# One more chunk of u through block transposes and DRAM instead of TensorE, and an early split of the last batch's slot weights

## The chip, the cores and the metric

The kernel runs on one core of a Trainium2 chip. The core has a matrix engine (PE, whose weight loads appear as PEld), a vector engine (DVE), a scalar engine (ACT), a GpSimd engine (POOL) and SyncE (SP), which here issues nearly all transfers. Each engine executes its own instructions strictly in program order and waits on semaphores for the others. The metric is the device time of one execution in microseconds (us).

## What is computed

A spectral layer (real FFT over 3072 positions, a complex linear layer with a soft threshold, the inverse FFT) for 8 batches of 3072 tokens of 256 features, then a soft mixture of experts with 32 slots, then a dense layer with softmax gating and a layer norm. The change lies in the last part. Cut to that part, the reference is:

```
c = softmax(logits, axis=1)           # tokens x 32 slots
x = c @ slot_out                      # tokens x 256
h = x @ w_in                          # tokens x 1024
u = h * softmax(h, axis=1)
ln = (u - mean(u)) / sqrt(var(u) + 1e-6) * g_ln
out = ln @ w_out                      # tokens x 256
```

Everything is float32. For the large products the kernel splits a factor into a high part, rounded to the matrix engine's reduced float32 form, and a low part, which is the remainder.

## The kernel before

Phase 1 (up to about 655 us of the trace) does the spectral layer, the logits and the slot inputs, and leaves in a DRAM tensor `c_dram` the slot weights `c` of each batch, transposed, as a high and a low part. The last batch is stored once, unsplit.

Phase 2, the function `phase2`, then walks over the 24576 tokens in 192 tiles of 128 tokens. `i` counts tiles, `j` is a group of four tiles, `k` is a tile's place in its group. I call four tiles a round. The loop at its end writes out by hand, per iteration `i`, which tile each step works on; that order is the order on every engine:

- `hmat(i+2)` on PE: two matmuls of 512 columns give `hps`, the 1024 values of h for 128 tokens. `expo(i+1)` on ACT, `rowmax(i+2)` and `umul(i+1)` on DVE give the row minimum (of the negated h), the exponential, and the product `u`.
- `trans(i)` on PE turns the first four 128-column chunks of `u` into PSUM (`pu`, two buffers): four transposes. `uhi(i)` on ACT copies them rounded into `uh` (L1068); `ulo(i)` on DVE subtracts and writes `ul` (L1077).
- `blocks(i+1)` is the other way for the last four chunks. DVE transposes 32x32 blocks into `tb` (L1049), SP writes `tb` to DRAM as `td` (L1051). `sort(i)` reads it back (L1060), in an order that completes the transpose, into `t2`; the profile calls that tile `t`. Since `sort(i)` stands behind `blocks(i+1)`, a tile's read is issued after the next tile's write. `uhl2(i-2)` on POOL makes the high and the low part from it: a cast (L1086) and a subtraction (L1087).
- `vari(i)` on ACT squares; `rstd(i)` on POOL makes the scale factors, five small instructions once a round; `outp(i-4)` on ACT scales the result into `osb`, and once a round POOL adds its halves into `os` (L1143), which SP stores.
- `prod(i-3)` on PE: eight matmuls of 512 columns with the chunks of `uh`, then eight of 256 columns with the chunks of `ul`.

On POOL the order at a round's last iteration (`i%4 == 3`) is `uhl2` of the round's second tile, `rstd`, `os`; then `uhl2` of the third, the fourth, and the next round's first tile. I call the tile whose `uhl2` stands ahead of `rstd` and `os` A, and the one behind them B.

MB is the number of chunks that go by DRAM (4), MA the number that PE transposes. The rows of `w_out` lie in `wout_dram` in an order that depends on MB, written in phase 1 by `dec_rows` during the decoding of the weights. The last three tiles (`direct`) send no chunk through DRAM: POOL reorders the last four chunks into `ts` (L1046) and PE transposes them too, as a second group with the second `pu` buffer.

`pieces(j+2)` gives `hmat` the slot weights. For batches 0 to 6 they come from `c_dram` already split. For the last batch POOL makes the split in phase 2, per group: one cast of 128x512 (L978) and two subtractions of 32x512 (L981).

Of the kernel before, what the change touches and what calls it, by code (L numbers as in the profile page):

```python
# [35 lines left out]
def kernel(  # L36
# [99 lines left out]
    MB = 4  # L136
# [12 lines left out]
    def phase1(pl: ExitStack, pr_: ExitStack):  # L149
# [560 lines left out]
        def dec_rows(f, k, n, c):  # L710
            if n < MA:
                SP.dma_start(out=wout_dram[128 * n:128 * n + 128], in_=f[:, n - k, :])
                return
            v = wout_dram[128 * MA:1024].rearrange("(i b c) d -> b c i d", b=4, c=MB)
            for c in (c, c + 1):
                SP.dma_start(out=v[n - MA, c], in_=f[32 * c:32 * c + 32, n - k, :])
# [131 lines left out]
    def phase2(p2: ExitStack, pw: ExitStack):  # L848
        k_p = p2.enter_context(tc.tile_pool(name="k2_p", bufs=1))
        c_p = p2.enter_context(tc.tile_pool(name="c_p", bufs=2))  # L850
# [7 lines left out]
        def load_c(b, h):  # L858
            if b >= B:
                return  # L860
            t = c_p.tile([128, 32, 32], F32R, name="ct", tag="ct", bufs=3)
            for k in range(4):
                SP.dma_start(out=t[32 * k:32 * k + 32].rearrange("s a j -> s (a j)").bitcast(F32), in_=c_dram[b, 0 if b == B - 1 else k % 2, h])
            cts[b, h] = t
# [103 lines left out]
        def pieces(j):  # L968
            if j >= NG:
                return  # L970
            b, r = divmod(j, 6)
            h, ah = divmod(r, 2)
            src = cts[b, h][:, 16 * ah:16 * ah + 16, :].rearrange("p a j -> p (a j)")
            ctt[j] = src
            if b == B - 1:
                src = src.bitcast(F32)
                c4 = ctt[j] = c_p.tile([128, 512], F32R, name="c4", tag="c4")
                POOL.tensor_copy(out=c4, in_=src)  # L978
                for k in (1, 3):
                    z = slice(32 * k, 32 * k + 32)  # L980
                    POOL.tensor_tensor(out=c4[z], in0=src[z], in1=c4[z].bitcast(F32), op=ALU.subtract)  # L981
            if ah:
                c_todo[4 * j + 3] = (b + 1, h)
# [44 lines left out]

        def trans(i):
            if i >= NI:  # L1030
                return
            u = ut[i]
            for n, v in enumerate([u, u2t[i]] if direct(i) else [u]):
                ps = pu_p.tile([128, 4, 128], F32, name="pu", tag="pu")
                for k in range(4):
                    tp(ps[:, k, :], v[:, k * 128:(k + 1) * 128])
                ut[i, n] = ps


        def blocks(i):  # L1040
# [3 lines left out]
            if direct(i):  # L1044
                t = u2t[i] = u_p.tile([128, 512], F32, name="ts", tag="ts", bufs=2)
                POOL.tensor_copy(out=t.rearrange("p (c i b) -> p c i b", c=MB, b=4), in_=v.rearrange("p (b c i) -> p c i b", b=4, c=MB))  # L1046
                return
            t = u_p.tile([128, 512], F32, name="tb", tag="tb", bufs=2)
            DVE.transpose(out=t, in_=v)  # L1049
            d = t_d.tile([128, 512], F32, name="td", tag="td")  # L1050
# [4 lines left out]
        def sort(i):  # L1055
# [3 lines left out]
            t2 = u_p.tile([128, 4, 128], F32, name="t2", tag="t2", bufs=3)  # L1059
# [3 lines left out]
        def uhi(i):  # L1063
            if i >= NI:
                return
            uh = u_p.tile([128, 8, 128], F32R, name="uh", tag="uh")
            for n in range(2 if direct(i) else 1):
                ACT.activation(out=uh[:, 4 * n:4 * n + 4, :], in_=ut[i, n], func=AF.Copy)  # L1068
            uht[i] = [uh]

        def ulo(i):
# [3 lines left out]
            for n in range(2 if direct(i) else 1):  # L1075
                z = slice(4 * n, 4 * n + 4)
# [74 lines left out]

        c_todo = {}
# [16 lines left out]
        for i in range(NI + 4):  # L1169
# [6 lines left out]
            late_c(i)  # L1176
            trans(i)
# [153 lines left out]
```

## Time and profile before

| | |
|---|---|
| median of 3 runs | 1393.14 us (1391.06 to 1394.41) |
| the profiled execution | 1393.42 us, of which the span of the trace 1391.6 us |
| busy, share of the span | PE 96%, DVE 87%, PEld 81%, ACT 75%, POOL 67% |
| chain that ended last | PE 78%, DVE 9%, POOL 4%, issue 4% |

Shares of the whole span mix two phases. Phase 2 alone, from about 680 us, shows PE and DVE nearly without idle time. A view by stretches shows how busy each engine is there, the chain of waits shows whose instructions follow one another without a gap, and the timeline shows how long before its use each piece is ready.

### The profile page before, as it was taken

The page shows a single profiled execution, that of the slowest core. Times are in us where ns is not written, and L with a number is a line of the kernel's source. Part 1 is how long each engine was busy: PE and PEld are TensorE (multiplying, and loading weights), DVE is VectorE, ACT ScalarE, POOL GpSimd, SP SyncE. Part 2 cuts the span into 40 slices and gives each one's busy share as a digit, 9 for nine tenths or more (in the row PEclk, how much of TensorE's full clock was granted, in tenths as well). Part 3 has the DMA queues.
Part 4 walks back from the last instruction along what each step waited for, and adds up shares of the span by engine and source line. Part 5 has one row for each costly group of instructions (what it writes and reads, how often), then busy time and mean ns, then how long its engine had stood idle before and what let it go on. Part 6 is the DMA issues. An engine that isn't in the chain of part 4 may idle for free.

```text
span 1391.6 us, 28564 instructions
## 1 busy us (share of the span) xinstructions
PE 1331.2 (96%) x10012; PEld 1132.7 (81%) x10012; DVE 1217.5 (87%) x1885; ACT 1045.7 (75%) x2006; POOL 929.9 (67%) x963
## 2 busy tenths in 40 slices
PE   6999999999999998977899999999999999999998
PEld 3888888888888887854788888888888888888786
DVE  6777988887888889756999999999999999999995
ACT  5557676757666664433899999999999999999885
POOL 5557575757575644320577877878878878879996
PEclk8899999999999999989799999999999999999999
DMA  8865473637364562286465566665666665666552
GB/s 268 282 194 170 129 206 106 209 88 206 114 195 125 168 208 75 76 285 199 137 207 187 190 204 198 194 200 190 199 193 206 198 193 186 205 195 193 180 167 84
DMA packets 207774, 250.84 MB, mean 180 GB/s; under 512 B 15536, under 2 KB 148400, under 8 KB 207632
## 3 DMA queue, kind: packets, MB, share of 16 engines
q1 hardware_dynamic: 207296, 247.84, 57.3%
q8 instruction: 80, 1.31, 0.4%
q10 hardware_dynamic: 336, 1.18, 0.3%
q14 instruction: 62, 0.51, 0.1%
HBM read 141.09 MB, written 107.87 MB: 179 GB/s over the span
## 4 chain that ended last, share of the span: by engine, by line
PE 78%; DVE 9%; POOL 4%; issue 4%; DMA 2%; ACT 2%; SPq 0%; DVEq 0%; POOLq 0%; ACTq 0%
PE po L89 36%; PE pb L89 8%; PE hps L89 6%; PE pm L89 6%; PE pu L92 5%; PE s L89 5%; PE xps L89 4%; PE pa L89 3%; PE sps L92 2%; DMA xc<-in_x_dram 2%; PE pm L92 1%; POOL x L238 1%; DVE sl L316 1%; DVE yb L343 1%; DVE yb L342 1%
## 5 line engine op out<-in xcount | busy, mean ns | idle before, releaser
L89 PE MATMUL po<-gw,uh 128*128 128x512 f32 x1536 | 407.5, 407 | 3.5 <-POOL uh L1086 3.5
L89 PEld LDWEIGHTS po<-gw,uh 128*128 128x128 f32 x1536 | 274.7, 189 | 57.1 <-POOL uh L1086 6.0
L346 POOL TENSOR_TENSOR s<-yb,s 128x512 f32<-128x512 f32 x95 | 132.3, 1393 | 215.9 <-DVE s L345 190.2
L1005 DVE TENSOR_REDUCE st<-hps 128x1 f32<-128x1024 f32 x192 | 235.1, 1225 | 30.0 <-PE hps L89 10.7
L1087 POOL TENSOR_TENSOR ul<-t,uh 128x512 fp32r<-128x512 f32 x189 | 244.5, 1294 | 15.2
L1020 DVE SCALAR_TENSOR_TENSOR u<-hps,e 128x1024 f32<-128x1024 f32 x192 | 233.3, 1215 | 1.4 <-ACT e L1012 1.4
L89 PEld LDWEIGHTS po<-gw,ul 128*128 128x128 f32 x1536 | 207.7, 188 | 17.8
L1095 ACT ACTIVATE sq<-u,st 128x1024 f32<-128x1024 f32 x192 | 219.5, 1143 | 0.0
L1012 ACT ACTIVATE e<-hps,st 128x1024 f32<-128x1024 f32 x192 | 213.9, 1114 | 2.9 <-DVE st L1005 2.9
L89 PE MATMUL po<-gw,ul 128*128 128x256 f32 x1536 | 210.6, 279 | 0.0
L1086 POOL CAST uh<-t 128x512 fp32r<-128x512 f32 x189 | 115.8, 613 | 135.7 <-DMA t<-td 107.6
L238 POOL TENSOR_TENSOR x<-xc,x 96x512 fp32r<-96x512 f32 x120 | 162.7, 1365 | 32.8 <-ACT x L237 30.2
L1068 ACT ACTIVATE uh<-pu 128x512 fp32r<-128x512 f32 x195 | 116.7, 599 | 67.8 <-PE pu L92 57.3
L1136 ACT ACTIVATE osb<-po,st 128x512 f32<-128x512 f32 x192 | 130.7, 681 | 9.7 <-PE po L89 6.9
L1077 DVE TENSOR_TENSOR ul<-pu,uh 128x512 fp32r<-128x512 f32 x195 | 133.7, 686 | 3.6 <-ACT uh L1068 3.6
L1049 DVE STREAM_TRANSPOSE tb<-u 128x512 f32<-128x512 f32 x189 | 132.7, 702 | 0.0
L264 ACT ACTIVATE asb<-s 96x512 f32<-96x512 f32 x112 | 66.6, 595 | 74.4 <-PE s L89 74.4
L92 PEld LDWEIGHTS pu<-ident,u 128*128 128x128 f32 x768 | 96.5, 141 | 26.1 <-issue 0.8
L92 PE MATMUL pu<-ident,u 128*128 128x128 f32 x768 | 116.6, 275 | 0.0
L89 PE MATMUL s<-x,df_h 96*96 96x512 f32 x240 | 104.7, 438 | 12.3 <-ACT x L237 4.7
L89 PE MATMUL hps<-gst,ct 128*128 128x512 f32 x336 | 106.7, 400 | 10.0 <-DVE u L1020 8.6
L1143 POOL TENSOR_TENSOR os<-osb 128x1024 f32<-128x1024 f32 x47 | 113.4, 2413 | 0.0
(205 smaller groups left out, 2587.8 us busy)
## 6 DMA issues: line engine op xcount, KB each, us to landing
td<-tb SPq DMA_DIRECT2D x189, 256.0 KB, 2.1
t<-td SPq DMA_DIRECT2D x189, 256.0 KB, 3.1
apt<-ad SPq DMA_DIRECT2D x96, 256.0 KB, 4.1
out_dram<-os SPq DMA_DIRECT2D x47, 512.0 KB, 3.8
xc<-in_x_dram SPq DMA_DIRECT2D x56, 384.0 KB, 4.0
ad<-asb SPq DMA_DIRECT2D x56, 384.0 KB, 3.5
ct<-c_dram SPq DMA_DIRECT2D x96, 128.0 KB, 3.5
wt<-in_moe_w_dram SPq DMA_DIRECT2D x21, 512.0 KB, 8.5
```

The costliest lines, as they stand in the source:

```text
L89: PE.matmul(out=out, lhsT=lhsT, rhs=rhs, start=start, stop=stop)
L92: PE.transpose(out=out, in_=in_, identity=ident[0:k, 0:k])
L238: POOL.tensor_tensor(out=lo, in0=t, in1=hi.bitcast(F32), op=ALU.subtract)
L346: (DVE if (b, t) == (B - 1, NT - 1) else POOL).tensor_tensor(out=s, in0=yb, in1=s, op=ALU.subtract)
L1005: DVE.tensor_reduce(out=st[:, 0, k:k + 1], in_=hps[i], op=ALU.min, axis=AX.X)
L1012: ACT.activation(out=e, in_=hps[i], func=AF.Exp, bias=st[:, 0, k:k + 1], scale=-1.0, accum_out=st[:, 1, k:k + 1])
L1020: DVE.scalar_tensor_tensor(out=u, in0=hps.pop(i), scalar=1.0, in1=et.pop(i), op0=ALU.mult, op1=ALU.mult, accum_out=st[:, 2, k:k + 1])
L1049: DVE.transpose(out=t, in_=v)
L1077: DVE.tensor_tensor(out=ul[:, z, :], in0=ut.pop((i, n)), in1=uht[i][0][:, z, :].bitcast(F32), op=ALU.subtract)
L1087: POOL.tensor_tensor(out=ul[:, MA:8, :].rearrange("p c (a j) -> p c a j", a=4), in0=v, in1=w.bitcast(F32), op=ALU.subtract)
L1095: ACT.activation(out=sq, in_=ut.pop(i), func=AF.Square, bias=st[:, 2, k:k + 1], scale=-float(DFF), accum_out=st[:, 3, k:k + 1])
L1136: ACT.activation(out=o[:, k], in_=pot.pop(i), func=AF.Copy, scale=stt[j][:, 4, k:k + 1])
```

## The change

MB goes from 4 to 5: PE transposes three chunks of a tile, DVE, DRAM and POOL handle five. `tb`, `td` and `t2` grow from 512 to 640 columns, the ACT copy and the DVE subtraction shrink from 512 to 384. `dec_rows` writes w_out's rows in the order for five chunks, in 20 small stores (16 before) and three large ones (four before), in one more of the decoding's steps. The three direct tiles now use groups of 3, 3 and 2 transposes, with the same two `pu` buffers. The split of the last batch's weights no longer happens per group in the last batch. A new function `last_c`, called right after `late_c(i)`, loads the unsplit weights at iteration 20, splits them in four pieces of 96x256 on POOL at iterations 24, 26, 28 and 30, and stores both parts to `c_dram` at 33; `load_c` then reads them as for any batch. The pool that held the per-group copies has one buffer.

```diff
-    MB = 4
+    MB = 5
...
-                SP.dma_start(out=v[n - MA, c], in_=f[32 * c:32 * c + 32, n - k, :])
+                SP.dma_start(out=v[divmod(4 * (n - MA) + c, MB)], in_=f[32 * c:32 * c + 32, n - k, :])
...
-                SP.dma_start(out=t[32 * k:32 * k + 32].rearrange("s a j -> s (a j)").bitcast(F32), in_=c_dram[b, 0 if b == B - 1 else k % 2, h])
+                SP.dma_start(out=t[32 * k:32 * k + 32].rearrange("s a j -> s (a j)").bitcast(F32), in_=c_dram[b, k % 2, h])
...
-            if b == B - 1:
-                src = src.bitcast(F32)
-                c4 = ctt[j] = c_p.tile([128, 512], F32R, name="c4", tag="c4")
-                POOL.tensor_copy(out=c4, in_=src)
-                for k in (1, 3):
-                    z = slice(32 * k, 32 * k + 32)
-                    POOL.tensor_tensor(out=c4[z], in0=src[z], in1=c4[z].bitcast(F32), op=ALU.subtract)
...
+        def groups(i):
+            return ((0, MA), (MA, 6), (6, 8)) if direct(i) else ((0, MA),)
...
-            for n, v in enumerate([u, u2t[i]] if direct(i) else [u]):
+            for n, (z0, z1) in enumerate(groups(i)):
+                v, o = (u2t[i], MA) if n else (ut[i], 0)
...
-            d = t_d.tile([128, 512], F32, name="td", tag="td")
+            d = t_d.tile([128, 128 * MB], F32, name="td", tag="td")
...
-            t2 = u_p.tile([128, 4, 128], F32, name="t2", tag="t2", bufs=3)
+            t2 = u_p.tile([128, 4, 32 * MB], F32, name="t2", tag="t2", bufs=3)
...
+        def last_c(i):
+            d = [c_dram[B - 1, k].rearrange("h s x -> (h s) x") for k in range(2)]
+            if i == 20:
+                cl[0] = o_p.tile([96, 1024], F32R, name="cl", tag="cl", bufs=1)
+                cl[1] = o_p.tile([96, 1024], F32R, name="cl_h", tag="cl_h", bufs=1)
+                SP.dma_start(out=cl[0].bitcast(F32), in_=d[0])
+            elif i in (24, 26, 28, 30):
+                z = slice(128 * (i - 24), 128 * (i - 24) + 256)
+                POOL.tensor_copy(out=cl[1][:, z], in_=cl[0][:, z].bitcast(F32))
+                POOL.tensor_tensor(out=cl[0][:, z], in0=cl[0][:, z].bitcast(F32), in1=cl[1][:, z].bitcast(F32), op=ALU.subtract)
+            elif i == 33:
+                SP.dma_start(out=d[0], in_=cl[1].bitcast(F32))
+                SP.dma_start(out=d[1], in_=cl[0].bitcast(F32))
...
             late_c(i)
+            last_c(i)
```

PE in an ordinary tile of phase 2, before (`pu` is `trans`, `po` is `prod`, with the chunks of `uh` and `ul` as weights):

```order
L92 MATMUL pu<-ident,u 128x128 [waits PE_49]
L92 MATMUL pu<-ident,u 128x128 x3
L89 MATMUL po_10523<-gw,uh 128x512 [waits PE_49,Activation_49]
L89 MATMUL po_10523<-gw,uh 128x512 x3
L89 MATMUL po_10523<-gw,uh 128x512 [waits Pool_49]
L89 MATMUL po_10523<-gw,uh 128x512 x3
L89 MATMUL po_10523<-gw,ul 128x256 x4
L89 MATMUL po_10523<-gw,ul 128x256 [waits Pool_49]
L89 MATMUL po_10523<-gw,ul 128x256 x3
```

The same place after:

```order
L92 MATMUL pu<-ident,u 128x128 [waits PE_49]
L92 MATMUL pu<-ident,u 128x128 x2
L89 MATMUL po_10505<-gw,uh 128x512 [waits PE_49,Activation_49]
L89 MATMUL po_10505<-gw,uh 128x512 x2
L89 MATMUL po_10505<-gw,uh 128x512 [waits Pool_49]
L89 MATMUL po_10505<-gw,uh 128x512 x4
L89 MATMUL po_10505<-gw,ul 128x256 x3
L89 MATMUL po_10505<-gw,ul 128x256 [waits Pool_49]
L89 MATMUL po_10505<-gw,ul 128x256 x4
```

One transpose is gone, and PE's waits for POOL moved from the fifth to the fourth matmul of each kind.

PE in a direct tile at the end of phase 2, before (`ts` is POOL's reordered copy):

```order
L92 MATMUL pu<-ident,u 128x128 [waits DVE_49]
L92 MATMUL pu<-ident,u 128x128 x3
L92 MATMUL pu<-ident,ts 128x128 [waits DVE_49,Pool_49]
L92 MATMUL pu<-ident,ts 128x128 x3
L89 MATMUL po_18237<-gw,uh 128x512 [waits Activation_49]
```

The same place after:

```order
L92 MATMUL pu<-ident,u 128x128 [waits DVE_49]
L92 MATMUL pu<-ident,u 128x128 x2
L92 MATMUL pu<-ident,ts 128x128 [waits DVE_49,Pool_49]
L92 MATMUL pu<-ident,ts 128x128 x2
L92 MATMUL pu<-ident,ts 128x128 [waits DVE_49]
L92 MATMUL pu<-ident,ts 128x128
L89 MATMUL po_18003<-gw,uh 128x512 [waits Activation_49]
```

A third group with a wait of its own for DVE now stands between the transposes and the product.

POOL in the last batch, before (`c` is the split of the slot weights):

```order
L1087 TENSOR_TENSOR ul<-t_16669,uh 128x512 [waits PE_49,Pool_49]
L978 CAST c_16775<-ct 128x512 [waits DMAHW0_49]
L981 TENSOR_TENSOR c_16775<-ct,c_16775 32x512 [waits Pool_49]
L981 TENSOR_TENSOR c_16775<-ct,c_16775 32x512
L1086 CAST uh<-t_16721 128x512 [waits DVE_49,DMAHW4_49,PE_49,Pool_49]
```

The same place after:

```order
L1083 TENSOR_TENSOR ul<-t_16525,uh 128x640 [waits PE_49,Pool_49]
L1082 CAST uh<-t_16576 128x640 [waits DMAHW2_49,DVE_49,PE_49]
L1083 TENSOR_TENSOR ul<-t_16576,uh 128x640 [waits PE_49,Pool_49]
L1082 CAST uh<-t_16622 128x640 [waits DMAHW5_49,DVE_49,PE_49]
L1083 TENSOR_TENSOR ul<-t_16622,uh 128x640 [waits PE_49,Pool_49]
```

The three instructions of the split are gone from there, and the cast and subtraction of each tile are 640 columns wide.

## Rows read from the trace of the kernel before

**Rows 1.** Stretches: length, busy PE, PEld, DVE, ACT, POOL, granted clock, DMA share

```profile
1000.00:1100.00 100.00, 100.00 (x597) 86.63 (x596) 97.08 (x136) 92.04 (x165) 80.24 (x96) 1.00 0.62 196
1300.00:1340.00 40.00, 37.87 (x222) 31.87 (x221) 35.89 (x51) 34.03 (x61) 37.80 (x43) 1.00 0.55 178
```

**Rows 2.** Chain that ended last: start, length, engine, tile, line, instructions

```profile
754.78 2.80 PE po L89 x16
...
1264.46 2.80 PE po L89 x16
```

**Rows 3.** The same chain at 746 us, the transposes of one tile

```profile
746.96 0.44 PE pu L92 x4
```

**Rows 4.** Costliest groups between 700 and 1380 us: busy, mean ns, idle before

```profile
L1087 POOL TENSOR_TENSOR ul<-t,uh 128x512 fp32r<-128x512 f32 x181 | 234.2, 1294 | 14.5
...
L89 PE MATMUL po<-gw,ul 128*128 128x256 f32 x1456 | 199.4, 279 | 0.0
...
L1077 DVE TENSOR_TENSOR ul<-pu,uh 128x512 fp32r<-128x512 f32 x185 | 126.8, 686 | 3.6 <-ACT uh L1068 3.6
L1049 DVE STREAM_TRANSPOSE tb<-u 128x512 f32<-128x512 f32 x178 | 124.9, 702 | 0.0
...
L1086 POOL CAST uh<-t 128x512 fp32r<-128x512 f32 x180 | 110.3, 613 | 86.3 <-DMA t<-td 58.3 <-PE hps L89 9.9 <-PE pu L92 9.0
L1143 POOL TENSOR_TENSOR os<-osb 128x1024 f32<-128x1024 f32 x45 | 108.6, 2413 | 0.0
```

**Rows 5.** Timeline of an ordinary round, tiles A and B: start, length, instruction

```profile
901.31 0.70 DVE L1049 STREAM_TRANSPOSE tb<-u 128x512 f32<-128x512 f32 x1
...
906.17 0.37 SPq L1060 DMA_DIRECT2D t<-td  x1
...
909.40 0.61 POOL L1086 CAST uh<-t 128x512 fp32r<-128x512 f32 x1 [1.58 <-DVE tb L1049]
...
916.03 0.61 POOL L1086 CAST uh<-t 128x512 fp32r<-128x512 f32 x1
...
916.72 1.29 POOL L1087 TENSOR_TENSOR ul<-t,uh 128x512 fp32r<-128x512 f32 x1
...
918.99 1.09 PE L89 MATMUL po<-gw,ul 128*128 128x256 f32 x8
```

**Rows 6.** DMA issues between 800 and 1200 us: size, us to landing

```profile
td<-tb SPq DMA_DIRECT2D x108, 256.0 KB, 2.1
t<-td SPq DMA_DIRECT2D x108, 256.0 KB, 3.1
out_dram<-os SPq DMA_DIRECT2D x28, 512.0 KB, 3.8
```

**Rows 7.** Timeline of a round in the last batch

```profile
1335.07 0.62 POOL L1086 CAST uh<-t 128x512 fp32r<-128x512 f32 x1
...
1339.61 2.64 POOL L981 TENSOR_TENSOR c<-ct,c 32x512 fp32r<-32x512 f32 x2
...
1350.83 0.62 POOL L1086 CAST uh<-t 128x512 fp32r<-128x512 f32 x1
...
1351.51 1.20 PE L89 MATMUL po<-gw,uh 128*128 128x512 f32 x4 [0.69 <-POOL uh L1086]
1351.53 1.31 POOL L1087 TENSOR_TENSOR ul<-t,uh 128x512 fp32r<-128x512 f32 x1
...
1352.55 1.11 PE L89 MATMUL po<-gw,ul 128*128 128x256 f32 x8
```

**Rows 8.** Timeline at the direct tiles

```profile
1364.77 1.09 POOL L1046 COPY ts<-u 128x512 f32<-128x512 f32 x1
...
1366.33 2.11 PE L89 MATMUL po<-gw,uh 128*128 128x512 f32 x8
...
1367.54 1.28 DVE L1077 TENSOR_TENSOR ul<-pu,uh 128x512 fp32r<-128x512 f32 x2
...
1369.61 1.08 POOL L1046 COPY ts<-u 128x512 f32<-128x512 f32 x1
```

More of the change, by code (lines that the diff above doesn't have):

```diff
@@ L849, in phase2 @@
         k_p = p2.enter_context(tc.tile_pool(name="k2_p", bufs=1))
-        c_p = p2.enter_context(tc.tile_pool(name="c_p", bufs=2))
+        c_p = p2.enter_context(tc.tile_pool(name="c_p", bufs=1))
         gw = k_p.tile([128, 8, 2, D], F32R, name="gw")
@@ L1031, in trans @@
                 return
-            u = ut[i]
-            for n, v in enumerate([u, u2t[i]] if direct(i) else [u]):
+            for n, (z0, z1) in enumerate(groups(i)):
+                v, o = (u2t[i], MA) if n else (ut[i], 0)
                 ps = pu_p.tile([128, 4, 128], F32, name="pu", tag="pu")
-                for k in range(4):
-                    tp(ps[:, k, :], v[:, k * 128:(k + 1) * 128])
-                ut[i, n] = ps
+                for k in range(z0, z1):
+                    tp(ps[:, k - z0, :], v[:, (k - o) * 128:(k - o + 1) * 128])
+                ut[i, n] = ps[:, 0:z1 - z0]
         def blocks(i):
@@ L1044, in blocks @@
             if direct(i):
-                t = u2t[i] = u_p.tile([128, 512], F32, name="ts", tag="ts", bufs=2)
+                t = u2t[i] = u_p.tile([128, 128 * MB], F32, name="ts", tag="ts", bufs=2)
                 POOL.tensor_copy(out=t.rearrange("p (c i b) -> p c i b", c=MB, b=4), in_=v.rearrange("p (b c i) -> p c i b", b=4, c=MB))
                 return
-            t = u_p.tile([128, 512], F32, name="tb", tag="tb", bufs=2)
+            t = u_p.tile([128, 128 * MB], F32, name="tb", tag="tb", bufs=2)
             DVE.transpose(out=t, in_=v)
-            d = t_d.tile([128, 512], F32, name="td", tag="td")
+            d = t_d.tile([128, 128 * MB], F32, name="td", tag="td")
             SP.dma_start(out=d, in_=t)
@@ L1066, in uhi @@
             uh = u_p.tile([128, 8, 128], F32R, name="uh", tag="uh")
-            for n in range(2 if direct(i) else 1):
-                ACT.activation(out=uh[:, 4 * n:4 * n + 4, :], in_=ut[i, n], func=AF.Copy)
+            for n, (z0, z1) in enumerate(groups(i)):
+                ACT.activation(out=uh[:, z0:z1, :], in_=ut[i, n], func=AF.Copy)
             uht[i] = [uh]
@@ L1074, in ulo @@
             ul = u_p.tile([128, 8, 128], F32R, name="ul", tag="ul")
-            for n in range(2 if direct(i) else 1):
-                z = slice(4 * n, 4 * n + 4)
+            for n, z in enumerate(groups(i)):
+                z = slice(*z)
                 DVE.tensor_tensor(out=ul[:, z, :], in0=ut.pop((i, n)), in1=uht[i][0][:, z, :].bitcast(F32), op=ALU.subtract)
@@ L1150, in store @@
                 SP.dma_start(out=v, in_=os2)
+        cl = {}
+        def last_c(i):
[11 more added lines that the diff above has]
+                SP.dma_start(out=d[1], in_=cl[0].bitcast(F32))
         c_todo = {}
```

## The prediction

> **What bounds the kernel now.** I read the busy time by stretches first, since shares of the whole span mix two phases. In the middle of phase 2 PE is busy 100.00 of 100 us at a granted clock of 1.00 (2.4 GHz), DVE 97.08, POOL 80.24 [rows 1]. So PE bounds an ordinary tile, and DVE has only about 0.1 us of idle time in a tile. The chain of waits agrees: it is PE's own instructions without a gap, 509.68 us for 138 tiles, 3.693 us a tile [rows 2], 14.77 us a round of four. In the last batch the picture is another one: PE is busy 37.87 of 40 us and POOL 37.80 [rows 1]. There POOL never rests: a round on POOL takes 1350.83 - 1335.07 = 15.76 us, and PE waits for POOL's cast inside its product [rows 7]. The five rounds of this kind in the last batch are 1.0 us longer than an ordinary one.
>
> The last thing I read is how early POOL is. In an ordinary round tile A's block transpose starts on DVE at 901.31, SP issues its read at 906.17, POOL starts on it at 909.40, then does `rstd` and `os`, starts tile B at 916.03 and ends B's subtraction at 916.72 + 1.29 = 918.01 [rows 5]. PE starts the eight `ul` matmuls of B at 918.99. The steps between them are (1.09 - 0.28) / 7 = 0.116 us, with 0.28 for the last one's own length [rows 4], so the fifth, the first that needs POOL's part, comes at 919.45. That is 1.44 us later. Of these some 0.18 us are a hand-over that remains where PE does wait: POOL ends at 1351.53 + 1.31 = 1352.84 and the fifth matmul comes at 1352.55 + 4 x 0.119 = 1353.03 [rows 7]. So **POOL is 1.26 us early at tile B**, and earlier at the others, since only B stands behind `rstd` and `os`.
>
> **What each part costs.**
>
> *PE, one transpose less.* Four take 0.44 us of the chain [rows 3], so one is 0.11 us a tile, and PE's round becomes 14.77 - 0.44 = 14.33 us. The products keep their sixteen matmuls.
>
> *DVE.* The subtraction loses 128 columns and the block transpose gains 128. By their rows of 512 columns [rows 4] that is at most -686/4 = -172 ns and +702/4 = +176 ns; with a fixed part in each both are smaller and still equal. DVE's 97.08 us of work in 100 is 3.585 us a tile, 14.34 us a round: level with the new PE round, so DVE takes nothing back by itself, but there is nothing more to gain below 14.34. ACT's copy gets shorter, off the path.
>
> *POOL.* The trace has the subtraction at 512 columns (1294 ns) and a two-input addition at 1024 (2413 ns) [rows 4]: 2.19 ns a column, 0.28 us for 128. In proportion to 1294 it would be 0.32. The cast has one size here (613 ns): 0.15 us in proportion, some 0.13 with the same fixed share. Together +0.41 to +0.48 us a tile; I take 0.44, the middle. Is POOL then the bound? Its full round of 15.76 less the last batch's split (2.64 for its two subtractions and a 128x512 cast like L1086's 0.61 ahead of them, 3.3) is 12.4 us [rows 7]; plus 4 x 0.44 gives 14.2. It just fits into 14.34.
>
> *Transfers.* Write and read grow by 64 KB. The write is covered, because a read is issued only after the next tile's write. The read's 3.1 us [rows 6] lie on POOL's path. Bounds for the growth: nothing, if the same number of longer packets takes the same time, and 0.78 us in proportion to size. The nearest rows are the SP stores of 256 KB (2.1) and 512 KB (3.8) [rows 6], 0.42 us for 64 KB if all of it is transfer; the DMA engines are busy 0.62 of the time [rows 1], so a part is idle capacity. I take 0.25. The Trainium skill ("DMA: Bandwidth & Descriptors", "Anatomy of one DMA") gives about 2.0 us and bytes over 436 GB/s, which is 0.15 us for 64 KB and 2.6 us for 256 KB; the store of 256 KB here takes 2.1, so the trace does not carry that fit. With 0.15 the sum below would end at 1384.
>
> *POOL's lead at tile B.* All of this meets in the 1.26 us. POOL now does two longer tiles (A and B) between the read and the use: -0.88. The read lands later: -0.25. PE needs the data sooner: from A's block transpose to B's `ul` matmuls lie five PE periods, each 0.11 shorter; one comes back since the read waits for the next tile's write, one period later (-0.44). B's own transposes are one fewer (-0.11), and the first chunk from POOL is the fourth, not the fifth (-0.12). Sum -1.80: the lead becomes **-0.54 us, so PE waits**. A wait of PE in one round moves that round's PE times by as much, but the next round's tile A was transposed before it, so the next deadline is later by the same amount: lateness 0.54 is paid about every other round, 0.27 us a round on average. What is late next is B's `ul`; behind the waiting matmul on PE stand the next `hmat` and, through it, DVE and ACT. The round becomes 14.33 + 0.27 = 14.60 us.
>
> *The last batch's split.* Its 3.3 us a round go, and with them the five rounds that are 1.0 us longer: -5.0. In their place come four casts and four subtractions of 96x256, by half the cast (0.31) and 1.29 - 0.56 for the subtraction about 1.04 us each pair, 1.12 with the gaps that POOL's rows show between instructions, 4.5 us in two rounds. Two of the four pairs stand directly ahead of a tile B. POOL's room is 14.60 - 14.2 = 0.4 us a round; some 1.1 us are absorbed by the time it has caught up, and 3.4 us reach PE (bounds 2.0 and 4.5). The three transfers of 384 KB are issued by SP ahead of a write and a read; I count them in that range.
>
> *The tail.* A direct tile now has three groups for two PSUM buffers, so the third must wait until DVE has subtracted the first. Before, the second group is through and the product starts at 1366.33, while DVE does the two subtractions of that tile only from 1367.54 [rows 8], behind the next `umul`. The first ends 0.64 us later; then come the third group and the product, about 1368.4: +2.0 us. The next direct tiles also wait for POOL, whose copies lie 4.84 us apart [rows 8] and will lie 0.27 (the copy) + 0.44 further apart; by the third that is about 2.1 in all, not on top of the first. I take 2.1 (bounds 1.0 and 3.5).
>
> *Phase 1.* Four more small stores on SP, one more decoding step: no wait of another engine hangs on them, nothing.
>
> **Sum.** About 45 rounds times (14.60 - 14.77) = -7.7; the split out of the last batch -5.0; the early split +3.4; the tail +2.1. Together -7.2 us on the profiled execution's 1393.42, which is 0.28 above the median: **1386 us**.
>
> **Rivals.**
>
> *All hidden.* If POOL's lead is larger than I make it (the read no slower, PE's wait not formed), the round is 14.34, DVE's bound: 45 x -0.43 = -19.4, -5.0, +2.5 with more room on POOL, +2.1: 1374. For it: POOL's demand of 14.2 fits. Against: even with no slower read and 0.41 a tile the lead is 1.26 - 0.82 - 0.67 = -0.23.
>
> *Given back exactly.* A wait of 0.44 a round (lateness 0.88) leaves the round at 14.77; -5.0, then +3.4 to 4.5 and +2.1 remain: 1394.
>
> *Slower: POOL's path becomes longer than PE's old round.* With 0.48 a tile and a read 0.78 slower, the lead is 1.26 - 0.96 - 0.78 - 0.67 = -1.15, the wait 0.57, the round 14.90: 45 x 0.13 = +5.9, -5.0, +4.5 as POOL has no room, +3.5: 1402. It decides from a lateness of about 0.95 on. For it: the read's landing varies between tiles and a late one at A is paid in full. Against: no row shows 64 KB costing so much. The Trainium skill ("GPSIMD Engine Reference", "Engine selection") speaks against moving elementwise work to this engine, about twice as slow with two inputs; the same 512-column subtraction takes 1294 ns on POOL and 686 on DVE here, so the trace agrees on the engine's time. By that rule this rival would be the rule's outcome, 1402.
>
> **Chances.** Forecast (1380 to 1390) 0.47, hidden 0.20, given back 0.16, slower 0.17. About 0.2% (2.8 us) is what a measurement of this kernel can tell from no change; so faster 0.66, same 0.17, slower 0.17. The range 1375 to 1400 takes in most of the hidden case and of the slower one, and leaves out about 0.2.
>
> **What would show it.** Right: PE's chain in phase 2 shows three transposes a tile and a wait for POOL's `ul` at tile B, some 0.3 us a round, often in alternate rounds; the last batch's rounds are like the others; POOL is busy 95% or more; around tiles 24 to 31 PE loses 2 to 4 us; a direct tile's third group waits for DVE. A round of 14.34 without waits of PE would show the lead mis-sized. Longer `t` reads than 3.4 us, or a subtraction over 1.6 us, would show the slower case. Wrong altogether: a DVE whose 640-column transpose costs much more than 0.88 us would make DVE the bound.

## The result: 0.6% slower, and where the time went

The changed kernel takes 1400.0 us (median of five runs, 1398.34 to 1401.76), the kernel before 1392.14 in the same comparison: a ratio of 1.0057, 95% interval 1.0042 to 1.0071. The forecast was 1386, and the direction was wrong. The profiled execution took 1401.76 us, with a span of 1400.0.

The page of the kernel after: busy time and share of the span by engine, then the chain that ended last by engine.

```profile
PE 1326.8 (95%) x9823; PEld 1114.6 (80%) x9823; DVE 1218.4 (87%) x1888; ACT 1027.2 (73%) x2009; POOL 986.9 (70%) x953
...
PE 54%; DVE 17%; POOL 12%; DMA 7%; issue 6%; ACT 4%; SPq 0%; POOLq 0%; DVEq 0%; ACTq 0%
```

PE has 189 matmuls less, and yet the chain is no longer PE's own: PE's share fell from 78% to 54%, and POOL and DMA, which were at 4% and below, are now 12% and 7%. The same two stretches as in [rows 1], after (columns as there):

```profile
1000.00:1100.00 100.00, 98.77 (x569) 83.76 (x568) 96.13 (x136) 88.35 (x163) 89.45 (x96) 1.00 0.74 229
1300.00:1340.00 40.00, 39.73 (x231) 33.83 (x230) 38.51 (x54) 35.20 (x65) 35.81 (x39) 1.00 0.66 211
```

In the middle of phase 2 PE now has idle time; POOL went from 80 to 89, the DMA engines from 0.62 to 0.74. In the last batch the loss is gone (PE 37.87 to 39.73). The waits between 700 and 1390 us (engine, line, releaser, us in total, times, longest) name the ones that have grown:

```profile
POOL uh L1082 <- DMA t<-td: 31.2, 38, 2.5
DVE st L998 <- PE hps L89: 25.9, 35, 1.8
PEld po L89 <- POOL uh L1082: 25.0, 34, 1.9
PE po L89 <- POOL uh L1082: 10.9, 17, 1.4
```

The same three of DVE and PE in the kernel before, between 700 and 1380 us:

```profile
DVE st L1005 <- PE hps L89: 6.5, 7, 1.1
PEld po L89 <- POOL uh L1086: 6.0, 6, 1.1
PE po L89 <- POOL uh L1086: 3.5, 5, 0.7
```

PE waits for POOL's cast, and DVE then waits for PE's `hps`, as the prediction had it behind the waiting product. An ordinary round of after, tiles A and B as in [rows 5] (timeline: start, length, engine, line, instruction, idle time before it):

```profile
908.45 0.83 DVE L1045 STREAM_TRANSPOSE tb<-u 128x640 f32<-128x640 f32 x1
...
913.33 0.37 SPq L1056 DMA_DIRECT2D t<-td  x1
...
917.28 0.72 POOL L1082 CAST uh<-t 128x640 fp32r<-128x640 f32 x1 [0.66 <-DMA t<-td]
...
921.94 2.41 POOL L1139 TENSOR_TENSOR os<-osb 128x1024 f32<-128x1024 f32 x1
...
924.30 0.72 POOL L1082 CAST uh<-t 128x640 fp32r<-128x640 f32 x1
...
925.07 1.00 PEld L89 LDWEIGHTS po<-gw,uh 128*128 128x128 f32 x5 [0.33 <-POOL uh L1082]
925.10 1.58 POOL L1083 TENSOR_TENSOR ul<-t,uh 128x640 fp32r<-128x640 f32 x1
...
926.35 1.25 PE L89 MATMUL po<-gw,ul 128*128 128x256 f32 x8
```

A's block transpose starts at 908.45 and POOL has A's data at 917.28, 8.83 us later; before it was 909.40 - 901.31 = 8.09 [rows 5]. POOL is idle for 0.66 us until then, works without a gap through `rstd`, `os` and B, and ends B's subtraction at 925.10 + 1.58 = 926.68. B's eight `ul` matmuls, of which the last five need it, have begun at 926.35 and take 1.25 us in place of 1.09.

Where the 8.3 us of the two spans come from, worked out as the start of the same tile's first product in the one trace and the other:

| stretch | change, us | forecast |
|---|---|---|
| up to tile 4 (phase 1 and start) | +2.73 | 0 |
| tiles 4 to 20 | +0.03 | -0.7 |
| tiles 20 to 40 (early split) | +4.51 | +2.5 |
| tiles 40 to 160 (30 rounds) | +3.10 | -5.1 |
| tiles 160 to 185 (last batch) | -5.55 | -6.0 |
| tiles 185 to 188 (direct tiles) | +3.55 | +2.1 |
| the rest | -0.04 | 0 |

Over tiles 48 to 151 a PE period without a wait is 3.594 us (3.693 before), so a round without waits would be 14.374. The round is 14.863: a wait of 0.49 us a round, where the forecast had 0.27.

### The profile page after: what moved, and what is told of

The parts are those of the page before. It is cut to its first block, busy times and chain, and to the rows that moved or that the text cites. A ratio compares the mean times of both kernels' runs of the same rounds, so it can differ in the third digit from the quotient of the medians.

```text
span 1400.0 us, 28198 instructions
## 1 busy us (share of the span) xinstructions
PE 1326.8 (95%) x9823; PEld 1114.6 (80%) x9823; DVE 1218.4 (87%) x1888; ACT 1027.2 (73%) x2009; POOL 986.9 (70%) x953
## 4 chain that ended last, share of the span: by engine, by line
PE 54%; DVE 17%; POOL 12%; DMA 7%; issue 6%; ACT 4%; SPq 0%; POOLq 0%; DVEq 0%; ACTq 0%
PE po L89 20%; PE pb L89 7%; PE pm L89 6%; PE s L89 5%; POOL os L1139 4%; PE xps L89 4%; DMA t<-td 3%; PE hps L89 3%; DVE u L1013 3%; PE pa L89 3%; DVE st L998 3%; DMA xc<-in_x_dram 3%; POOL ul L1083 2%; POOL uh L1082 2%; PE sps L92 2%
## 5 line engine op out<-in xcount | busy, mean ns | idle before, releaser
L89 PE MATMUL po<-gw,uh 128*128 128x512 f32 x1536 | 415.8, 410 | 11.9 <-POOL uh L1082 11.2
L1083 POOL TENSOR_TENSOR ul<-t,uh 128x640 fp32r<-128x640 f32 x189 | 297.2, 1573 | 15.2
L89 PE MATMUL po<-gw,ul 128*128 128x256 f32 x1536 | 216.1, 282 | 0.0
L1082 POOL CAST uh<-t 128x640 fp32r<-128x640 f32 x189 | 136.1, 720 | 84.1 <-DVE tb L1045 44.8
L1064 ACT ACTIVATE uh<-pu 128x384 fp32r<-128x384 f32 x198 | 97.0, 490 | 91.0 <-PE pu L92 84.9
L1045 DVE STREAM_TRANSPOSE tb<-u 128x640 f32<-128x640 f32 x189 | 157.8, 835 | 0.0
L89 PE MATMUL hps<-gst,ct 128*128 128x512 f32 x384 | 122.0, 400 | 10.6 <-DVE u L1013 9.2
L1073 DVE TENSOR_TENSOR ul<-pu,uh 128x384 fp32r<-128x384 f32 x198 | 108.9, 550 | 5.0 <-ACT uh L1064 4.8
L89 PEld LDWEIGHTS xps<-d_sb,apt 128*128 128x128 f32 x768 | 99.6, 194 | 13.5 <-issue 2.9
L89 PE MATMUL xps<-d_sb,apt 128*128 128x128 f32 x768 | 106.0, 281 | 1.4 <-DMA apt<-ad 1.3
```

Source lines behind the costliest of these rows:

```text
L89: PE.matmul(out=out, lhsT=lhsT, rhs=rhs, start=start, stop=stop)
L1082: POOL.tensor_copy(out=w, in_=v)
L1083: POOL.tensor_tensor(out=ul[:, MA:8, :].rearrange("p c (a j) -> p c a j", a=4), in0=v, in1=w.bitcast(F32), op=ALU.subtract)
```

## The experiments

All medians, each against the kernel before on the same chip; "wait" is the round over tiles 48 to 151 less four PE periods without a wait (14.374, or 14.773 with four chunks); the next two columns are changes against the kernel before in the traces.

| kernel | median us | ratio (95%) | wait a round | tiles 20 to 40 | tiles 185 to 188 |
|---|---|---|---|---|---|
| after | 1400.0 | 1.0057 (1.0042, 1.0071) | 0.49 | +4.51 | +3.55 |
| e1_five_only | 1412.3 | 1.0137 (1.0114, 1.0159) | 0.53 | +0.77 | +2.65 |
| e2_early_only | 1388.8 | 0.9961 (0.9948, 0.9973) | 0.00 | +0.97 | -0.16 |
| e3_short_read | 1392.3 | 0.9990 (0.9978, 1.0001) | 0.25 | +4.79 | +3.57 |
| e4_os_later | 1382.2 | 0.9917 (0.9898, 0.9936) | 0.18 | +2.25 | +3.55 |
| e5_split_start | 1378.0 | 0.9881 (0.9866, 0.9895) | 0.12 | -0.49 | +3.26 |
| e6_two_groups | 1378.2 | 0.9887 (0.9870, 0.9903) | 0.12 | -0.74 | +3.84 |
| e7_short_pool | 1390.1 | 0.9966 (0.9953, 0.9979) | 0.21 | +4.93 | +2.65 |
| e8_long_read | 1394.5 | 1.0009 (0.9998, 1.0021) | 0.01 | 0.00 | +0.16 |
| e9_spread_c | 1377.4 | 0.9886 (0.9870, 0.9902) | 0.01 | -0.24 | +3.56 |
| e10_tail | 1373.5 | 0.9862 (0.9848, 0.9875) | 0.04 | -1.01 | +0.90 |
| e11_store_k0 | 1376.1 | 0.9881 (0.9867, 0.9895) | 0.04 | +0.01 | +0.91 |
| e12_four_best | 1389.2 | 0.9975 (0.9963, 0.9987) | 0.05 | +1.09 | +0.36 |
| e13_dec_steps | 1373.1 | 0.9850 (0.9830, 0.9869) | 0.05 | +0.38 | +0.94 |

**The two parts apart.** e1 is the changed kernel with the old split of the last batch:

```diff
+            if b == B - 1:
+                src = src.bitcast(F32)
+                c4 = ctt[j] = c_p.tile([128, 512], F32R, name="c4", tag="c4")
+                POOL.tensor_copy(out=c4, in_=src)
...
-            last_c(i)
```

> The first part of the change alone: five chunks by DRAM, but the last batch's weights are split per group in the last batch, as before. In the changed kernel the steady rounds were about 0.1 us longer than before (tiles 40 to 160: +3.1 us in 30 rounds), the tail cost +3.5, the start +2.7. If the early split is what cost the +4.5 us around tiles 20 to 40, those go here; the last batch has POOL at about 13.95 + 3.3 = 17.25 us a round against 15.76 before, five rounds, +7.5. Sum by this reading: 1392 + 2.7 + 4 (rounds) + 7.5 + 3.5, about 1407 to 1410. Rival, that the longer rounds come from somewhere else than POOL's path (PE or DVE): the last batch then costs no more than before, and the time is about 1392 + 2.7 + 4 + 3.5 = 1402.

Measured 1412.3, above the 1407 to 1410 expected: the last batch lost 9.9 us in place of 7.5. The +4.5 of tiles 20 to 40 go to +0.77 without the early split, and in the last batch tiles 160 to 185 take 9.86 us longer than before. That is 107.4 us for 6.25 rounds, 17.2 a round, which is POOL's own work as expected (17.25). A stretch of the last batch in e1 (columns as in [rows 1]):

```profile
1300.00:1340.00 40.00, 35.96 (x197) 28.85 (x196) 34.12 (x47) 30.91 (x56) 37.84 (x40) 1.00 0.55 175
```

POOL is as busy there as before (37.80), and PE falls from 37.87 to 35.96. So five chunks need the early split, or lose more than they win.

e2 has MB = 4 and direct groups `((0, MA), (MA, 8))`, with `last_c`.

> The second part alone: four chunks by DRAM as before, the last batch's weights split early. POOL is 1.26 us ahead of PE at tile B before, and a pair of early pieces takes 0.40 + 0.73 = 1.13 us on POOL in the changed kernel. If the +4.5 us around tiles 20 to 40 were POOL's lateness, the pieces are hidden here: 1392 - 5.0 + 0 to 1.5, that is 1387 to 1389. If the three transfers of 384 KB cost it (by holding up the reads), some 2 to 4 us of it remain: 1389 to 1391. If the +2.7 us at the start of the changed kernel come from the early split's side (its loads or stores in phase 1), they show here too; by the reading that they vary from kernel to kernel without a cause in phase 2, they need not.

Measured 1388.8: -5.17 us in the last batch, as forecast, and +0.97 at tiles 20 to 40. The POOL pieces are nearly hidden where POOL has a lead: of the 0.97 us, 0.25 lie in the round from tile 24 on and 0.72 in the round from tile 32 on, whose transfers stand behind the two stores of 384 KB. The same pieces and stores cost 4.1 in the changed kernel (4.51 less the ordinary 0.09 a round). Over an ordinary wait of 0.49, the rounds from tiles 20, 24 and 28 on are there 1.36, 1.34 and 0.26 us longer and the round behind the stores 1.60, while the next one waits for nothing. So more than a third of the cost comes with the stores and not with POOL's pieces. The timeline shows PE's weight loads waiting behind the two pieces that stand directly ahead of a tile B:

```profile
759.46 1.00 PEld L89 LDWEIGHTS po<-gw,uh 128*128 128x128 f32 x5 [1.85 <-POOL uh L1082]
775.70 0.98 PEld L89 LDWEIGHTS po<-gw,uh 128*128 128x128 f32 x5 [1.87 <-POOL uh L1082]
```

**The read's length and POOL's work apart.** e3 reads 512 of the 640 columns, into one of three tiles that were filled with zeros once:

```diff
-            t2 = u_p.tile([128, 4, 32 * MB], F32, name="t2", tag="t2", bufs=3)
-            SP.dma_start(out=t2, in_=d.rearrange("(a i) (b x) -> (i b) a x", a=4, b=4))
+            t2 = t2s[i % 3]
+            SP.dma_start(out=t2[:, :, 0:128], in_=d.rearrange("(a i) (b x) -> (i b) a x", a=4, b=4)[:, :, 0:128])
...
```

> The changed kernel, but the read from DRAM fetches only 512 of the 640 columns (the rest of the tile keeps zeros, so a fifth of five chunks is left out of the result); the write, POOL's cast and subtraction, DVE and PE keep their sizes. Theory 'the read lands later': A's data came 0.77 us later than in the kernel before against PE's need, and the wait of 0.47 us a round is half of a lateness of 0.93. With a read of the old size the lateness falls to between 0.16 and 0.43, the wait to 0.08 to 0.22, 0.25 to 0.39 us a round less in some 43 rounds: 1400 - 11 to 17, that is 1383 to 1389. Rival 'POOL's own work': if POOL has no room left (13.95 us of work a round), the earlier data only make POOL idle elsewhere and the time stays within 1397 to 1401.

Measured 1392.3, 7.7 under the changed kernel: a larger gain than the rival allowed (1397 to 1401) and a smaller one than the theory said (1383 to 1389). The round is 0.24 us shorter, just under the theory's 0.25 to 0.39, and the early split's cost did not shrink with it.

e8 is the opposite: the kernel before, moving 640 columns:

```diff
-            d = t_d.tile([128, 512], F32, name="td", tag="td")
+            d = t_d.tile([128, 640], F32, name="td", tag="td")
...
-            t2 = u_p.tile([128, 4, 128], F32, name="t2", tag="t2", bufs=3)
+            t2 = u_p.tile([128, 4, 160], F32, name="t2", tag="t2", bufs=3)
...
```

> The kernel before with transfers of 640 columns: the block transpose, PE and POOL keep their 512 columns, but write and read move 128x640 (a fifth of it zeros; the columns are not in the right places for the result). It measures the read's growth alone. Theory 'the landing grows by itself, with bytes and load': the median from issue to landing goes from 3.1 to 3.5 or 3.6, A's data come 0.4 to 0.7 later, the lead at B falls from 1.26 to 0.6 to 0.9, and PE still does not wait: 1391.5 to 1394.5. Rival 'the read is later because PE's waits delay its issue': the landing stays within 0.15 of before. If the time itself rises by over 3 us, the larger traffic costs something that no theory here has.

Measured 1394.5 (ratio 1.0009, interval with 1.0 in it): no change of the time, since POOL's lead covers it. Its transfers between 800 and 1200 us (size, us from issue to landing), to hold against [rows 6]:

```profile
td<-tb SPq DMA_DIRECT2D x108, 320.0 KB, 2.4
t<-td SPq DMA_DIRECT2D x108, 320.0 KB, 3.7
out_dram<-os SPq DMA_DIRECT2D x27, 512.0 KB, 4.5
```

The changed kernel has the same 2.4 and 3.7. For tile A alone, the mean of 26 reads from issue to landing is 3.16 us before, 3.82 in e8, 3.90 in the changed kernel and 3.35 in e3. So nearly all of the read's growth (0.66 of 0.74) comes with the bytes: it needs no wait of PE and no longer POOL work. e8 enlarges the write too; e3, with the larger write and the old read, tells them apart: 0.55 of the 0.74 go with the read's own size.

e7 is the complement of e3: full transfers, but POOL handles only four chunks.

```diff
-            v = t2t.pop(i).rearrange("p a (c j) -> p c a j", c=MB)
+            v = t2t.pop(i).rearrange("p a (c j) -> p c a j", c=MB)[:, 1:MB]
...
```

> The changed kernel with its full transfers, but POOL casts and subtracts only four of the five chunks (512 columns); the product uses the fifth chunk in place of the fourth, which is left out of the result. The complement of e3, where the read alone was shortened (landing 0.4 to 0.55 us earlier, round 0.26 shorter). Theory 'the two terms add up to one lateness': POOL's two tiles between A's landing and B's end shorten by 2 x 0.386, the lateness falls from 0.93 to 0.16, the wait from 0.47 to about 0.1 a round, 0.37 x 43 = -16; with POOL's room the early split costs 1 to 2 in place of 4.5, -3; sum 1381, range 1379 to 1386. Rival 'a floor of DVE and PE': e4 without POOL's order stayed at 14.55 a round, so the round comes down by 0.29 at most: 1400 - 12 - 3 = 1385 or more.

Measured 1390.1, 9.9 under the changed kernel, where the theory said 14 to 21. The wait fell to 0.21, not 0.1, and tiles 20 to 40 still cost 4.93. The round came down by 0.28, which is also what the rival, a floor of DVE and PE near 14.55, allowed (0.29); e9's round of 14.38, below, rules that floor out. The 4.93 are mostly one event: the round from tile 32 on takes 5.08 us more than without waits, and without this the early split would cost about 1 us, as the theory had it (1 to 2). Behind the two stores of 384 KB at iteration 33 the writes of tiles 34 and 35 take 5.88 and 4.81 us (2.4 otherwise), their reads go out late, PE waits, and then runs at a lower clock:

```profile
796.00:800.00 4.00, 3.47 (x20) 2.56 (x18) 3.42 (x6) 1.31 (x3) 3.50 (x7) 1.00 0.81 261
800.00:803.00 3.00, 0.96 (x3) 0.48 (x3) 1.63 (x2) 2.75 (x5) 3.00 (x3) 1.00 0.65 187
803.00:808.00 5.00, 4.84 (x20) 4.25 (x21) 1.94 (x5) 2.25 (x6) 4.76 (x6) 0.66 0.71 236
```

PE is busy for 0.96 of 3 us, and in the next 5 us the granted clock is 0.66 in the mean, between the levels of 2.4 and 1.2 GHz. The same round of the changed kernel takes only 2.09 us more.

**POOL's order.** e4 moves one instruction of 2.41 us on POOL behind tile B:

```diff
-                POOL.tensor_tensor(out=os2, in0=o[:, :, 0, :], in1=o[:, :, 1, :], op=ALU.add)
-                o_todo[i + 2] = (v, os2)
+                os_wait.append((i, v, o))
...
+        def addh():
+            if os_wait:
...
+                POOL.tensor_tensor(out=os2, in0=o[:, :, 0, :], in1=o[:, :, 1, :], op=ALU.add)
+                o_todo[i + 3] = (v, os2)
...
             uhl2(i - 2)
+            addh()
```

> The changed kernel, but the once-a-round addition that makes os on POOL (2.41 us) stands behind tile B's cast and subtraction, no longer ahead of them; its store goes out one iteration later. Nothing else. Theory 'lateness at one tile': POOL has 13.95 us of work in a round of 14.37, so it fits; only B was late, by 0.93. B now gains 2.41 us, the next tile loses 2.41 and gains a tile period 3.59 and still has about 0.3 to spare. The waits go, the round is 14.37 (four PE periods of 3.59), 0.47 less in some 43 rounds: 1380, range 1377 to 1385. Rival 'POOL has no room': the wait moves from B to the tile behind it and the time is 1396 to 1401. Rival 'DVE is the floor': waits go from the chain, but the round stays at 14.6 or more, as DVE's own work and its waits fill it: 1389 to 1393.

Measured 1382.2: the range of the first theory, 18 us under the changed kernel and 11 under the kernel before, with the same work on every engine. The ordinary stretch (columns as in [rows 1]):

```profile
1000.00:1100.00 100.00, 100.00 (x584) 85.94 (x584) 99.48 (x140) 91.96 (x167) 92.20 (x96) 1.00 0.77 236
```

Its waits between 850 and 1260 us:

```profile
PEld po L89 <- POOL uh L1082: 5.0, 10, 0.9
```

The same in the changed kernel:

```profile
PEld po L89 <- POOL uh L1082: 14.0, 23, 1.1
```

Between 1000 and 1100 us PE is busy 100 of 100 us again, with POOL at 92 and DVE at 99.5; between 1100 and 1200 it is 99.3. The round over tiles 48 to 151 is 14.55, not 14.37: the waits that are left fall into every second round (0.36 us in an odd round, 0.00 in an even one). Those are the rounds in which SP issues the four loads of the next slot weights, and there the reads of the third and fourth tile mostly take 5 to 6 us.

e9 spreads these loads (after e5, which follows):

```diff
-                load_c(*c_todo.pop(i))
...
+                    c_part.extend((b, h, k) for k in range(4))
+            if c_part:
+                b, h, k = c_part.pop(0)
+                SP.dma_start(out=cts[b, h][32 * k:32 * k + 32].rearrange("s a j -> s (a j)").bitcast(F32), in_=c_dram[b, k % 2, h])
```

> The kernel e5_split_start with the four transfers of 128 KB that load the next slot weights issued one per iteration, in four iterations, in place of all four in one. In e4 and e5 PE's wait for POOL falls only in every second round, the rounds in which these loads are issued (in e4 0.36 us in an odd round, 0.00 in an even one; in e5 0.23 and 0.00), and there the reads of the third and fourth tile take 5 to 6 us in place of 3.3 to 3.9. Theory 'the loads hold up the reads': the waits of odd rounds go for the most part, 0.115 us a round in some 40 rounds, -3 to -5: 1373 to 1375. Rival 'the 512 KB store of the output does it', one iteration ahead of them and unchanged here: less than 1.5 us is won, 1376.5 to 1379.

In the trace the theory holds: between 850 and 1260 us the wait is 0.3 us in all, where e5, which differs only in these loads, has 3.2. The 512 KB store, the rival, is unchanged.

```profile
PEld po L89 <- POOL uh L1082: 0.3, 2, 0.2
```

The round is 14.38. The median (1377.4, runs from 1374.0 to 1379.1) does not show it against e5's 1378.0 and lies in the rival's range (1376.5 to 1379): from tile 4 to the end the profiled execution gains 2.94 us, and its tile 4 comes 3.45 us later than in e5. By time alone e9 is open, by the waits it is shown.

**The early split.** e5 is e4 with the split in the time in which POOL does nothing (627 to 667 us):

```diff
-            elif i in (24, 26, 28, 30):
...
+            if i < 0:
+                cl[0] = o_p.tile([128, 768], F32R, name="cl", tag="cl", bufs=1)
...
+        last_c(-1)
         hmat(0)
```

> The kernel e4_os_later, but the last batch's weights are loaded and split before the first tile of phase 2, in one cast and one subtraction over 128x768; the stores stay at iteration 33. In e4 POOL does nothing from 627 to 667 us. Theory 'the early split costs what POOL does not have': tiles 20 to 40 of e4 lost 2.25 us against the kernel before, where the rounds around them gain about 1.0; with the two instructions (some 0.9 + 1.9 us) in the idle time, that 3.3 us goes: 1382.2 - 3.3 = 1379, range 1377.5 to 1380.5. Rival 'the three transfers of 384 KB cost it': two of them still fall at tile 33, so more than half stays: 1381 to 1382.5.

The two instructions on POOL in e5's timeline, behind 28.79 us without work:

```profile
655.78 0.82 POOL L1164 CAST cl_h<-cl 128x768 fp32r<-128x768 f32 x1 [28.79 <-DMA cl<-c_dram]
656.69 1.81 POOL L1165 TENSOR_TENSOR cl<-cl,cl_h 128x768 fp32r<-128x768 f32 x1
```

Measured 1378.0, 4.2 under e4. Tiles 20 to 40 go from +2.25 to -0.49, so POOL's pieces were the larger part. The stores at iteration 33 stayed; with ordinary waits taken off they cost 0.9 here.

**The direct tiles.** e6 makes two groups in place of three:

```diff
-            return ((0, MA), (MA, 6), (6, 8)) if direct(i) else ((0, MA),)
+            return ((0, 4), (4, 8)) if direct(i) else ((0, MA),)
```

> The kernel e5_split_start, but a direct tile makes two groups of four transposes (the fourth of the first group from ts) in place of three groups of 3, 3 and 2. Theory 'the third group waits for DVE': in e4 the third groups wait 2.07 and 0.65 us for DVE's subtraction; the waits go. POOL then sets the tail: its copies ts lie 5.47 us apart in e4 (4.84 before), so 1.3 us of the tail's 3.55 stay, and 2.2 go: 1.5 to 2.5 us less than e5. Rival 'POOL sets the tail already': less than 0.7 us is won.

Measured 1378.2, nothing won: the wait for DVE went, and a longer one for POOL's copy came (timeline at the second direct tile):

```profile
1355.55 1.33 PE L92 MATMUL pu<-ident,ts 128*128 128x128 f32 x5 [3.83 <-POOL ts L1042]
1356.53 3.76 PE L89 MATMUL po<-gw,uh 128*128 128x512 f32 x8
```

The product takes 3.76 us in place of 2.11 [rows 8]; the granted clock between 1355.5 and 1360 us was 0.50, after 3.83 us without an instruction of PE. So the tail needs POOL's order mended as well. e10 is e9 with e6's two groups and that: the last `os` but one goes two iterations later, behind the copies (`i + 5` is its place in e4).

```diff
-                os_wait.append((i, v, o))
+                os_wait.append((i + 7 if j == NG - 3 else i + 5, v, o))
```

> The kernel e9_spread_c with two changes of the tail: two groups of four transposes in a direct tile, as in e6, and the last os but one (2.39 us on POOL, ahead of the copies ts that PE waits for) moved two iterations later, behind them. e6 alone won nothing: its wait for DVE (2.09) went, and PE waited 3.83 us for ts instead. Theory 'POOL's order sets the tail': ts(190) and ts(191) come 2.4 us earlier and PE's waits for ts (1.55 and 1.53 in e5, 3.83 in e6) shrink by about that: 2 to 4 us less than e9. Rival 'POOL's sum sets it', since its last work must be done anyway: less than 1 us.

Measured 1373.5, 3.9 under e9; in the traces tiles 185 to 188 go from +3.56 to +0.90, and all from tile 4 on is 2.1 shorter. The later `os` with the three groups kept was not run. The waits for `ts` are 1.50 us each, and the products take their 2.12 again:

```profile
1348.81 0.76 PE L92 MATMUL pu<-ident,ts 128*128 128x128 f32 x5 [1.50 <-POOL ts L1042]
1349.33 2.12 PE L89 MATMUL po<-gw,uh 128*128 128x512 f32 x8
```

e11 is e10 with `o_todo[i] = (v, os2)` in place of `o_todo[i - 2]`, the output's store two iterations later:

> The kernel e10_tail with the 512 KB store of the output two iterations later, at the first tile of a round in place of the third. If the store's collision with the reads of the third and fourth tile still makes PE wait there, the rest of the waits goes, up to 2 us. If the spread loads have taken the waits away, it is within 1 us of e10. If the store now holds up the read of the first tile and through it the second, where POOL starts its chain of work, it is slower by 1 to 4 us.

Measured 1376.1, 2.6 slower, but not for the reason that I gave. The waits a round are the same (0.04). In the trace 1.2 us come at the very end, behind the last products, where the late store is now among the last things done; 1.0 us more lies at tiles 20 to 40. Whether that is the store I leave open.

**What the fifth chunk is worth.** e12 is the kernel before with e5's split and e9's loads.

> The counterpart with four chunks by DRAM: the kernel before with the split at the start of phase 2 (as in e5) and the spread loads (as in e9). It tells what the fifth chunk is worth once its side effects are mended. PE's chain bounds its rounds at 14.77, so only the last batch's five rounds get shorter: 1393 - 5.0 - 0 to 0.7, that is 1387 to 1389; the fifth chunk is then worth the difference to e9, some 13 us less what the tail takes. If it comes below 1385, the reads cost the kernel before more than its chain shows.

Measured 1389.2, just above the 1387 to 1389 expected. The best kernel, e13 below, is 16 us faster, and e10, measured beside e12, 15.7. From tile 4 to tile 185 its trace gains 16.8 us on that of e12, and the direct tiles give back 0.6. So five chunks are worth some 15 us, once POOL's order, the split, the loads and the tail suit them. e12 has neither e4's order nor e10's tail; its waits are 0.05 a round and its direct tiles lose 0.4 us, so these could give it little.

**Phase 1.** e13 is e10 with the decoding back at its old number of steps:

```diff
-                    for q in range(0, 4, 2 if n >= MA else 4):
+                    for q in range(0, 4, 2 if n > MA else 4):
...
-            for c in (c, c + 1):
+            for c in range(4) if n == MA else (c, c + 1):
```

> The kernel e10_tail, but the four small stores of the first of the five chunks of w_out go out in one decoding step, so that the decoding has as many steps as with four chunks. Between 424 and 565 us of the trace all eight kernels with five chunks lose 1.1 to 2.2 us against the kernel before, those with four chunks 0.2 (e2: 0.76 to 0.93, e12: -0.98 to -0.76). Theory 'the extra step': each later decoding instruction on DVE falls one place further on, where PE waits for DVE; the loss in that stretch goes to 0.5 or less. Rival 'the stores': there are still 20 small stores in place of 16, two more of them in one burst, and the loss stays at 1 us or more. The median is expected 1 to 2 us under e10's 1373.5, which the scatter of phase 1's first 100 us may hide.

Between 424 and 565 us e13 gains 1.23 us on the kernel before, with all 20 small stores; the ten kernels with five chunks and the additional step (I had counted eight) lose 1.0 to 2.2 there, the three others with four chunks 0.2. So it is the step, and not the stores. How it costs the time, by pushing each later decoding instruction on DVE one place further, is argued and not shown, and why e13 gains more than the kernels with four chunks stays open. The median (1373.1) cannot tell it from e10's.

## Why the prediction failed, step by step

- **What bounds the kernel** was right: PE, with POOL's lead at tile B as the margin. e8 shows the margin directly: 0.66 us more on the read, and no change.

The groups of the kernel after between 700 and 1380 us, to hold against [rows 4] (columns as there):

```profile
L1083 POOL TENSOR_TENSOR ul<-t,uh 128x640 fp32r<-128x640 f32 x182 | 286.2, 1573 | 14.6
...
L1045 DVE STREAM_TRANSPOSE tb<-u 128x640 f32<-128x640 f32 x179 | 149.5, 835 | 0.0
L1082 POOL CAST uh<-t 128x640 fp32r<-128x640 f32 x181 | 130.3, 720 | 37.0 <-DMA t<-td 31.2 <-PE pu L92 2.2 <-DVE st L998 1.7
...
L1073 DVE TENSOR_TENSOR ul<-pu,uh 128x384 fp32r<-128x384 f32 x184 | 101.5, 552 | 1.2 <-ACT uh L1064 1.2
```

- **PE, DVE, POOL** held. The period fell by 0.10 us, not 0.11. DVE's transpose rose by 133 ns (835 against 702) and its subtraction fell by 134 (552 against 686). POOL's cast and subtraction rose by 107 and 279 ns, 0.39 a tile against the 0.44 taken: just below the lower bound of 0.41.
- **The read is the step that failed.** I took 0.25 from bounds of 0 and 0.78, because the DMA engines had idle capacity. It measured 0.74 at tile A. With this and POOL's 0.39 the prediction's own sum gives 1.26 - 0.77 - 0.74 - 0.67 = -0.92, and half of it is 0.46 us a round: 0.49 was measured. The rule that half of a lateness is paid stood; four rounds from tile 96 on, one by one, wait 0.03, 0.97, 0.00 and 0.85 us. By that rule the read's 0.74 in place of 0.25 alone is worth half of the difference a round, some 11 us over 45 rounds, of the 15.5 us between the forecast's -7.2 and the +8.3 of the two spans. A lateness of 0.92 lies between the rival "given back exactly" (0.88) and the slower one (from 0.95 on); the round came out as the slower one, 14.86, since the wait was 0.49 and four PE periods 14.37 and not 14.33. The Trainium skill's fit ("DMA: Bandwidth & Descriptors", "Anatomy of one DMA"), which the page gives for transfers issued by GpSimd and not by SP, yields an estimate of 0.15, further off.
- **The half rule near zero.** e3 and e7 bring the lateness to about -0.37 and -0.20, half of which is 0.19 and 0.10; they wait 0.25 and 0.21. A's landing scatters by some 0.2 to 0.4 us (standard deviation), and a read that is late is paid while an early one gives nothing back. A lead has to exceed the scatter before the waits go. I had named the scatter as a point for the slower rival, but not put it into the sum.
- **The last batch's split** was right (-5.0): e2, which has it alone, gains 5.17 there.
- **The early split** was within its bounds: 4.1 against 3.4. The waits are at B, but 1.6 us come in the round behind the two stores, which the prediction counted only in its range; e2, with room on POOL, pays 1.0 for the same instructions.
- **The tail** was right in kind, low in size: +3.55 against 2.1 and just over the upper bound of 3.5. The third group's wait was named. What was not: that PE's waits there lower its granted clock (0.60 between 1373 and 1377 us), so that a product took 3.26 us in place of 2.12.

```profile
1372.18 0.55 PE L92 MATMUL pu<-ident,ts 128*128 128x128 f32 x3 [1.79 <-POOL ts L1042]
...
1373.18 3.26 PE L89 MATMUL po<-gw,uh 128*128 128x512 f32 x8
```

- **Phase 1 at nothing** was wrong by about 1.1 us: the additional decoding step. The rest of the +2.73 is not the change's: 2.8 us arise between 72 and 102 us of the trace, where both kernels execute the same instructions, and the other traces move there by -1.1 to +0.9; what made it there is open.
- **The rivals.** The slower one came true in its mechanism, POOL's path longer than PE's old round, through the term that I thought least likely; 0.17 was too low a chance for a case that hung on one unmeasured transfer. That its 1402 came near is in part luck: it had a lateness of 1.15, where the measured terms give 0.92, and 2.7 us of the measured loss were there before tile 4. Of its signs the read over 3.4 us came (3.7) and the subtraction over 1.6 did not (1.573). The forecast saw that POOL's work fits and that B is late behind `rstd` and `os`; what it did not see is that a change of this order alone would turn the sign. POOL was busy 89 of 100 us, where 95 or more had been named as a sign, and moving one addition of 2.41 us turned +8 into -11.

## What to carry to other kernels

Price a longer transfer at its full proportion when it lies on the path to a waiting engine, even where the DMA engines look partly idle; in this one case 25% more bytes took 21 to 23% more time from issue to landing. When an engine has enough room but one of its results is late, look first at what stands ahead of that result in its queue: work with slack should go behind work without. And look at a lead against the scatter of what feeds it, not only against zero; bulk loads that share its queue are best issued in small pieces.

## What the runs showed of the hardware

- The read's time grew with its size although the DMA share was only 0.62 before: 3.16 to 3.82 us from 256 to 320 KB (e8, same schedule), while the write of the same bytes grew from 2.1 to 2.4.
- Behind two stores of 384 KB in a row the next two writes of 320 KB, 2.4 us otherwise, took 5.88 and 4.81 us in e7, 5.28 and 3.05 in the changed kernel.
- PE's clock fell after idle stretches inside otherwise dense work: to 0.66 after 3 us with 0.96 us busy (e7), and to 0.50 after 3.83 us of nothing (e6). The work behind such a wait then costs up to 1.8 times its time (3.76 against 2.11 us for eight matmuls). A wait of 1.50 us in e10 left the products at their 2.12 us.
